# Attention by values and its output transposes as 64x64 products in four places of the array

## The chip, the cores and the metric

The kernel runs on one core of one Trainium2 chip. The metric is the device time of one execution in microseconds. TensorE (PE in the profile) multiplies; VectorE (DVE), ScalarE (ACT) and GpSimd (POOL) work on SBUF and PSUM; SyncE (SP) issues the data transfers.

## What is computed

A delta-rule recurrence over 768 positions for 4 batches of 8 heads of dimension 48, and behind it a causal softmax attention with four experts (head dimension 64), whose outputs are mixed by a top-2 gate:

```python
for t in range(S):                       # first stage, k_n is k over its norm
    y[:, :, t] = einsum('bhd,bhde->bhe', q[:, :, t], state)
    v_old = einsum('bhde,bhd->bhe', state, k_n[:, :, t])
    state += beta[t] * outer(k_n[:, :, t], v[:, :, t] - v_old)
x = y with the heads side by side        # 4 x 768 x 384
for e in range(4):                       # second stage
    q, k, v = x @ wq[e], x @ wk[e], x @ wv[e]
    a = softmax(causal(q @ k.T / 8))
    out += gate[e] * (a @ v @ wo[e])     # gate: top 2 of x @ w_gate, softmax over the two
```

All inputs, and the products that the change touches, are float32.

## The kernel before

The work is cut into six units `n` (0 to 5) of 256 positions of two batches `b`; `s = n % 3` is the place of the unit in its sequence, so that its queries see the keys of `s + 1` units. The recurrence of a unit goes in four chunks of 64 positions, by products of 64x64 or smaller (steps `gk`, `gq`, `ks`, `uu`, `st`, `yq`, `yu`); these already stand in four places of the array, one for each half of its rows and half of its columns, and `turns` puts them in the order (0,0), (1,1), (0,1), (1,0). The triangular solve of each unit (`pre`, `pa`, `sv`; lines L422 and L420 in the profile) is a chain on DVE and POOL.

The attention of unit `n` follows the unit's recurrence and is interleaved with that of the next unit. For a batch `b`, a pair `y` of experts (`x` = 0, 1 within it) and a block `kp` of 256 keys:

- `sc` puts the transposed scores, keys on partitions, into a pair of PSUM banks, with a mask product where `kp == s`;
- `xp` (ACT, L743) takes the exponent into one of three SBUF tiles `at`;
- `av` multiplies by the values `VS`, 64 columns and a column of ones for the row sums, and adds over `kp` in PSUM: 128 keys by 128 queries a product, 65 moving columns. A block below the diagonal has 8 products, a block on it 6. A float32 product leaves two records in the trace, a load and a matmul each;
- `oa`, when all `kp` are done, copies the 128x260 sums from PSUM to `OS` (ACT for e = 0, 13 times; DVE for e = 1, 11 times), and this frees the pair of banks.

When all of a batch's experts are done, `nm` (three small DVE rows on `rsm`) and `on` (POOL or DVE) normalise and gate, `ft` transposes through the array against the identity, `fh` and `fl` evict in two parts, `fo` multiplies by `wo`, `eo` evicts and `do` stores.

PSUM is four pairs of two banks, `PP[0]` to `PP[3]` (`ps_65` to `ps_68` in the order of instructions). `two(k)` is pair `k`, with the bank as its second index. The order of all steps, and the pair or engine that each uses, is written out by hand in the table `ORDER`; every engine runs its own steps in that order, and waits on semaphores for the others.

Of the kernel before, what the change touches and what calls it, by code (L numbers as in the profile page):

```python
# [12 lines left out]
OP = mybir.AluOpType  # L13
# [10 lines left out]
SIDES = (slice(0, 64), slice(64, 128))  # L24
# [148 lines left out]
def tile_kernel(ctx, tc, kq, kv, beta, wqk, wvg, wo, consts, out):  # L173
    nc = tc.nc
    V, S, G, T = nc.vector, nc.scalar, nc.gpsimd, nc.tensor
# [5 lines left out]
    def mm(o, a, b, start, stop=True):  # L181
        T.matmul(o, lhsT=a, rhs=b, start=start, stop=stop, skip_group_check=True)  # L182

    def cpy(e, o, x, scale=None):
        if e == 0:
            S.activation(o, x, AF.Copy, **({} if scale is None else {"scale": scale}))  # L186
        elif scale is None:
            V.tensor_copy(o, x)
        else:
            V.tensor_scalar(o, x, scale, None, op0=OP.mult)  # L190
# [6 lines left out]
    def two(k):  # L197
        return PP[int(k)]
# [15 lines left out]
    id64 = cst[:, 0:64]  # L214
# [19 lines left out]
    VS = cp.tile([128, 2, 6, NE, EH + 1], F32, name="vs")  # L234
# [11 lines left out]
    OS = [cp.tile([128, NE, 2, EH + 1], F32, name=f"os{i}") for i in range(2)]  # L246
    ON = cp.tile([128, 2, NE, EH], F32, name="on")
# [415 lines left out]
    FOUR = ((0, 0), (1, 1), (0, 1), (1, 0))  # L663
# [81 lines left out]
    def av(n, b, y, kp, k):  # L745
        s = n % 3
        A = at_of(n, b, y, kp)
        O = two(k)[:, 0, 0:260].rearrange("p (x i d) -> p x i d", x=2, i=2)
        for j in range(2):
            for x in range(2):  # L750
                for i in range(j if kp == s else 0, 2):
                    o = 256 * j + 128 * i - (128 if kp == s and j else 0)
                    mm(O[:, x, i], A[:, x, o:o + 128], VS[:, b, 2 * kp + j, 2 * y + x], kp == j == x == i == 0)

    def oa(n, b, y, e, k):
        cpy(e, OS[b][:, 2 * y:2 * y + 2].rearrange("p x i d -> p (x i d)"), two(k)[:, 0, 0:260])

    def nm(n, b):
        rs = rsm[:, b]
# [8 lines left out]
    def ft(n, b, k):  # L768
        for i in range(2):
            for x in range(2):  # L770
                for r in range(2):
                    w = 128 * i + 64 * x
                    mm(two(k)[:, r, w:w + 64], ON[SIDES[r], i, 2 * x:2 * x + 2].rearrange("p e d -> p (e d)"), id64[SIDES[r]], True)

    fv = lambda k: two(k)[:, :, 0:256].rearrange("p r (q t) -> p q r t", q=4)
    ov = lambda x: x.rearrange("p i x (r t) -> p (i x) r t", r=2)
# [103 lines left out]
```

## Time and profile before

| | |
|---|---|
| median of 3 runs | 488.77 us (484.72 to 489.02) |
| the profiled execution's own time | 488.29 us |
| its span, first to last instruction | 486.4 us |
| mean granted TensorE clock | 0.959 |
| PE busy | 433.9 us, 89% |
| weight loads (PEld) busy | 396.1 us, 81% |
| DVE busy | 313.6 us, 64% |
| ACT, POOL busy | 182.3 us and 170.8 us |
| the chain that ended last | PE 71%, DVE 15%, DMA 4%, ACT 4% |

Busy time on PE is the union of matmuls from start to modelled end, so that short products that overlap count once, and the last one's latency counts in full. A row of the kind "x44, 5.13" in the timeline is 44 such records that follow each other. "Idle before" with "issue" as its releaser is a stop for which the trace shows no semaphore.

### The profile page before, as it was taken

To read this page: it belongs to the slowest core of one execution; us is meant where nothing else is said; L and a number is where in the kernel's file an instruction comes from. 1 tells how busy PE (TensorE), PEld (TensorE's weight loads), DVE (VectorE), ACT (ScalarE), POOL (GpSimd) and SP (SyncE) were. 2 spreads that over 40 slices of the span, in tenths; PEclk is the share of its full clock that TensorE was granted. 3 is DMA by queue.
4 is the path that set the end of the run, shared out by engine and by line. 5 is a ranking of instruction groups with operands and counts; after the bars stand their busy time and mean duration, and the time that the engine had idled before them with its cause. 6 is when DMAs were issued, how large, how long until landed. Compare 5 with 4: busy or idle time off the path is not lost.

```text
span 486.4 us, 21099 instructions
## 1 busy us (share of the span) xinstructions
PE 433.9 (89%) x9543; PEld 396.1 (81%) x9543; DVE 313.6 (64%) x655; ACT 182.3 (37%) x349; POOL 170.8 (35%) x314
## 2 busy tenths in 40 slices
PE   5529888878999889998999999999999989999995
PEld 4529777867888769897888989999887879999994
DVE  3996769766679894776667485775677764642011
ACT  2516233532325542364352354173531122323331
POOL 1505744544474462404146342744601000011000
PEclk9999999868999996998699999999999989999999
DMA  8920343211303151120035120011403000000001
GB/s 187 236 71 13 91 119 102 49 36 47 105 11 107 34 167 52 52 67 1 3 100 150 35 53 1 1 36 37 144 16 110 19 3 18 2 34 15 20 1 66
DMA packets 15435, 29.33 MB, mean 60 GB/s; under 512 B 2801, under 2 KB 8945, under 8 KB 15345
## 3 DMA queue, kind: packets, MB, share of 16 engines
q1 hardware_dynamic: 15088, 27.59, 20.7%
q8 instruction: 75, 1.23, 1.1%
q10 hardware_dynamic: 256, 0.39, 0.3%
q14 instruction: 16, 0.12, 0.1%
HBM read 20.89 MB, written 4.72 MB: 53 GB/s over the span
## 4 chain that ended last, share of the span: by engine, by line
PE 71%; DVE 15%; DMA 4%; ACT 4%; issue 3%; SPq 1%; POOL 1%; DVEq 0%; ACTq 0%; POOLq 0%
PE ps L182 71%; DMA at<-in_wvg_dram 2%; ACT tt L186 1%; DVE bl L420 1%; DVE mx L684 1%; DVE tp L422 1%; DMA kq<-in_kq_dram 1%; DMA kv<-in_kv_dram 1%; DVE tn L452 1%; DVE ql L619 1%; SPq L596 1%; DMA xh<-xh 1%; DVE tt L190 1%; DVE xb L538 1%; DVE xh L590 1%
## 5 line engine op out<-in xcount | busy, mean ns | idle before, releaser
L182 PE MATMUL ps<-vs,at 128*128 128x65 f32 x672 | 80.1, 276 | 0.1
L182 PEld LDWEIGHTS ps<-vs,at 128*128 128x128 f32 x672 | 77.3, 192 | 1.8 <-ACT at L743 0.4
L422 POOL TENSOR_TENSOR tp<-bl 128x238 f32<-128x238 f32 (+13 forms) x90 | 44.0, 489 | 89.3 <-DVE bl L420 80.6
L743 ACT ACTIVATE at<-ps 128x768 f32<-128x768 f32 (+1 forms) x48 | 43.8, 919 | 50.0 <-PE ps L182 49.8
L684 DVE TENSOR_REDUCE mx<-ps 128x2 f32<-128x1024 f32 (+3 forms) x48 | 44.8, 952 | 13.9 <-PE ps L182 13.6
L420 POOL TENSOR_TENSOR bl<-bl,tp 128x238 f32<-128x238 f32 (+13 forms) x90 | 47.1, 523 | 7.1
L182 PE MATMUL ps<-kq 48*64 48x64 f32 x1536 | 38.2, 243 | 12.0 <-DVE tt L348 4.8
L182 PE MATMUL ps<-xh,wqkh 128*128 128x256 f32 x288 | 45.5, 294 | 2.9 <-DMA xh<-xh 1.8
L182 PEld LDWEIGHTS ps<-kq 48*64 48x64 f32 x1536 | 32.4, 154 | 16.0 <-issue 6.6
L182 PEld LDWEIGHTS ps<-xh,wqkh 128*128 128x128 f32 x288 | 38.6, 194 | 4.9 <-issue 2.0
L186 ACT ACTIVATE tt<-ps 32x256 f32<-32x256 f32 (+2 forms) x87 | 33.4, 384 | 17.1 <-PE ps L182 10.7
L182 PE MATMUL ps<-qh,kh 64*128 64x256 f32 x192 | 35.1, 357 | 1.1 <-DVE sb L562 1.1
L182 PE MATMUL ps<-kh,qh 64*128 64x512 f32 (+3 forms) x128 | 26.8, 439 | 3.5 <-DVE kl L619 2.1
L182 PE MATMUL ps<-ql,kh 64*128 64x256 f32 x192 | 28.2, 285 | 0.0
L182 PEld LDWEIGHTS <-ide 64*128 64x128 bf16 (+1 forms) x479 | 23.3, 103 | 5.9 <-issue 1.2
L182 PE MATMUL ps<-qh,kl 64*128 64x256 f32 x192 | 28.0, 283 | 0.0
L182 PE MATMUL ps<-mr,sel 64*128 64x256 bf16 x192 | 27.3, 276 | 0.0
L182 PE MATMUL ps<-wvgh,xh 128*128 128x260 f32 x144 | 25.4, 303 | 1.4 <-DVE pm L356 1.4
L182 PE MATMUL ps<-mask,ide 64*128 64x128 bf16 (+1 forms) x384 | 26.4, 217 | 0.0
L765 POOL TENSOR_TENSOR on<-os,rsm 128x512 f32<-128x512 f32 x9 | 9.4, 1048 | 46.1 <-DVE rsm L762 46.1
L182 PE MATMUL ps<-xh,wqkl 128*128 128x256 f32 x144 | 25.4, 286 | 0.0
L182 PEld LDWEIGHTS ps<-wvgh,xh 128*128 128x128 f32 x144 | 21.2, 204 | 2.0 <-DVE pm L356 1.6
(197 smaller groups left out, 915.9 us busy)
## 6 DMA issues: line engine op xcount, KB each, us to landing
kv<-in_kv_dram SPq DMA_DIRECT2D x24, 384.0 KB, 3.7
kq<-in_kq_dram SPq DMA_DIRECT2D x40, 192.0 KB, 3.6
out_dram<-ot SPq DMA_DIRECT2D x12, 384.0 KB, 2.9
xh<-xh SPq DMA_DIRECT2D x72, 32.0 KB, 2.5
kq<-in_kq_dram SPq DMA_DIRECT2D x12, 96.0 KB, 3.9
at<-in_wqk_dram SPq DMA_DIRECT2D x3, 256.0 KB, 3.8
kq<-in_kq_dram ACTq DMA_DIRECT2D x4, 96.0 KB, 4.0
at<-in_wvg_dram SPq DMA_DIRECT2D x1, 256.0 KB, 7.6
```

The costliest lines, as they stand in the source:

```text
L182: T.matmul(o, lhsT=a, rhs=b, start=start, stop=stop, skip_group_check=True)
L186: S.activation(o, x, AF.Copy, **({} if scale is None else {"scale": scale}))
L190: V.tensor_scalar(o, x, scale, None, op0=OP.mult)
L420: e.tensor_tensor(X[:, a:b, i + 1:], X[:, a:b, i + 1:], tv, op=OP.subtract)
L422: e.tensor_tensor(tv, R[:, :, i + 1:].to_broadcast([128, w, m]), X[:, a:b, i:i + 1].to_broadcast([128, w, m]), op=OP.mult)
L452: V.transpose(TN[n % 2].rearrange("p t l -> p l t"), BB[n % 2])
L538: V.tensor_tensor(XB.rearrange("p (a b) d -> p a (b d)", a=2), kv_of(n, c)[:, 1].rearrange("p (a b) d -> p a (b d)", a=2), ax(k), op=OP.su ...
L590: V.tensor_tensor(x, y, yv(n, c, k, 0)[0], op=OP.subtract)
L596: nc.sync.dma_start(x[r + HD:r + 64, :, i].bitcast(F32), x[r + 16 * i:r + 16 * i + 16, :, 3].bitcast(F32))
L684: V.tensor_reduce(d, two(k)[:, :, a:a + 128 * (k1 - k0)], axis=AX.X, op=OP.max)
L743: S.activation(at_of(n, b, y, kp)[:, :, 0:w], two(k)[:, :, 0:w], AF.Exp, scale=0.125)
L765: (V, G)[e - 1].tensor_tensor(ON, OS[b][:, :, :, 0:EH].rearrange("p e i d -> p i e d"), rsm[:, b, :, :, None].to_broadcast([128, 2, NE, EH ...
```

## The change

`av` cuts each 128x128 product into four of 64x64: key half `r` (rows of the array) by query half `c` (its columns). The two key halves go to the two banks of the pair, so both banks now hold a partial sum. On a diagonal block the products whose key half lies above the query half are left out, except in units 0 and 3, where one of each pair is still needed to write the region. The products of the four places take turns, in the same order of places as `turns` has. `oa` copies bank 0 as before, on the engine that it had, and then adds bank 1 on DVE. `ft` takes a 64x64 piece at a time where it took 64x128. `ORDER` is as it was.

```diff
     def av(n, b, y, kp, k):
         s = n % 3
         A = at_of(n, b, y, kp)
-        O = two(k)[:, 0, 0:260].rearrange("p (x i d) -> p x i d", x=2, i=2)
-        for j in range(2):
-            for x in range(2):
-                for i in range(j if kp == s else 0, 2):
-                    o = 256 * j + 128 * i - (128 if kp == s and j else 0)
-                    mm(O[:, x, i], A[:, x, o:o + 128], VS[:, b, 2 * kp + j, 2 * y + x], kp == j == x == i == 0)
+        O = two(k)[:, :, 0:260].rearrange("p r (x i d) -> p r x i d", x=2, i=2)
+        todo = {}
+        for x in range(2):
+            for j in range(2):
+                for i in range(2):
+                    for r in range(2):
+                        for c in range(2):
+                            if kp == s and 2 * j + r > 2 * i + c and (s or j):
+                                continue
+                            todo.setdefault((r, c), []).append((x, j, i))
+        seen = set() if kp == 0 else {(r, c) for r in range(2) for c in range(2)}
+        while any(todo.values()):
+            for r, c in ((0, 0), (1, 1), (0, 1), (1, 0)):
+                if not todo[r, c]:
+                    continue
+                x, j, i = todo[r, c].pop(0)
+                o = 256 * j + 128 * i + 64 * c - (128 if kp == s and j else 0)
+                mm(O[SIDES[c], r, x, i], A[SIDES[r], x, o:o + 64], VS[SIDES[r], b, 2 * kp + j, 2 * y + x], (r, c) not in seen)
+                seen.add((r, c))
 
     def oa(n, b, y, e, k):
-        cpy(e, OS[b][:, 2 * y:2 * y + 2].rearrange("p x i d -> p (x i d)"), two(k)[:, 0, 0:260])
+        o = OS[b][:, 2 * y:2 * y + 2].rearrange("p x i d -> p (x i d)")
+        cpy(e, o, two(k)[:, 0, 0:260])
+        V.tensor_tensor(o, o, two(k)[:, 1, 0:260], op=OP.add)
...
     def ft(n, b, k):
         for i in range(2):
             for x in range(2):
-                for r in range(2):
+                for r, c in FOUR:
                     w = 128 * i + 64 * x
-                    mm(two(k)[:, r, w:w + 64], ON[SIDES[r], i, 2 * x:2 * x + 2].rearrange("p e d -> p (e d)"), id64[SIDES[r]], True)
+                    mm(two(k)[SIDES[c], r, w:w + 64], ON[SIDES[r], i, 2 * x + c], id64[SIDES[r]], True)
```

On PE, in the second expert pair of batch 0 and the first of batch 1 of the last unit, `av` of three key blocks stands in a row (here a product counts once, not twice as in the trace; `at_112` to `at_114` are the three exponent tiles, `ps_66` and `ps_67` two pairs of banks):

```order
 L182 MATMUL ps_68<-mr_86,sel 128x256
-L182 MATMUL ps_66<-vs,at_113 128x65 x8
-L182 MATMUL ps_66<-vs,at_114 128x65 x6
-L182 MATMUL ps_67<-vs,at_112 128x65 x8
+L182 MATMUL ps_66<-vs,at_113 64x65 x32
+L182 MATMUL ps_66<-vs,at_114 64x65 x20
+L182 MATMUL ps_67<-vs,at_112 64x65 x32
 L182 MATMUL ps_65<-qh_100,kh 128x256 x2
```

22 products become 84 in the same place between the same neighbours; nothing is moved.

On DVE, at the end of the program, the last two `oa` of batch 1 (`os_119`) and what waits behind them; L771 is the new addition:

```order
 L188 COPY os_119<-ps_67 128x260
+L771 TENSOR_TENSOR os_119<-os_119,ps_67 128x260
 L188 COPY ot<-ps_67 128x768
 L188 COPY os_119<-ps_68 128x260
-L760 TENSOR_SCALAR rsm<-os_119 128x8
-L761 RECIPROCAL rsm<-rsm 128x8
-L762 TENSOR_TENSOR rsm<-gt_127,rsm 128x8
-L765 TENSOR_TENSOR on<-os_119,rsm 128x512
+L771 TENSOR_TENSOR os_119<-os_119,ps_68 128x260
+L775 TENSOR_SCALAR rsm<-os_119 128x8
+L776 RECIPROCAL rsm<-rsm 128x8
+L777 TENSOR_TENSOR rsm<-gt_127,rsm 128x8
```

The additions stand directly behind the copies, ahead of the small rows of `nm` (L775 to L777, before L760 to L762).

On DVE, in the middle of the program, the row of unit 0 where one of the two evictions was ACT's (`os_118` from `ps_65`), between the copy and the solver's rows:

```order
 L188 COPY os_118<-ps_67 128x260
+L771 TENSOR_TENSOR os_118<-os_118,ps_67 128x260
+L771 TENSOR_TENSOR os_118<-os_118,ps_65 128x260
 L422 TENSOR_TENSOR tp<-bl_94 128x238
 L420 TENSOR_TENSOR bl_94<-bl_94,tp 128x17x14
```

DVE had no row for the eviction from `ps_65`; it now has one, which waits for the copy by ACT, with the solver's rows (L422, L420) queued behind it.

## The prediction

> **What bounds the kernel now.** I read the page first: which engine is busy, and what the chain that ended last is made of.
>
> ```profile
> PE 433.9 (89%) x9543; PEld 396.1 (81%) x9543; DVE 313.6 (64%) x655; ACT 182.3 (37%) x349; POOL 170.8 (35%) x314
> q8 instruction: 75, 1.23, 1.1%
> PE 71%; DVE 15%; DMA 4%; ACT 4%; issue 3%; SPq 1%; POOL 1%; DVEq 0%; ACTq 0%; POOLq 0%
> L182 PE MATMUL ps<-vs,at 128*128 128x65 f32 x672 | 80.1, 276 | 0.1
> ```
>
> The products by values are PE's costliest group, 80.1 us. An average over 486 us says little about what they are worth, so I then asked for the busy time by stretches, of all engines, and of these products alone:
>
> ```profile
> 0.00:240.00 240.00, 199.78 (x5026) 179.66 (x5030) 176.28 (x360) 96.73 (x206) 106.48 (x197) 0.93 0.30 79
> 240.00:300.00 60.00, 58.24 (x1302) 54.16 (x1294) 39.50 (x91) 24.94 (x44) 26.23 (x51) 1.00 0.25 69
> 300.00:400.00 100.00, 94.96 (x2314) 86.36 (x2313) 69.87 (x146) 35.06 (x66) 31.52 (x48) 0.98 0.16 45
> 400.00:480.00 80.00, 78.70 (x913) 74.05 (x910) 27.38 (x59) 24.80 (x34) 6.55 (x18) 1.00 0.06 19
> ...
> 0.00:240.00 240.00, 22.95 (x324) 0.93 0.30 79
> 240.00:300.00 60.00, 18.82 (x160) 1.00 0.25 69
> 300.00:400.00 100.00, 11.44 (x92) 0.98 0.16 45
> 400.00:480.00 80.00, 33.97 (x288) 1.00 0.06 19
> ...
> 399.95 76.08 PE ps L182 x880
> 476.06 0.44 DVE os L188
> ```
>
> Columns are length, then busy time and count of PE, PEld, DVE, ACT, POOL, then clock and transfers. The last two rows are from the chain in order of time. From 400 us on PE is the bound without a break: 76 us of the chain are PE alone, and DVE has 27 us to do in 80. Here a microsecond saved on PE is one saved at the end. Before 240 us PE is busy 200 of 240 and DVE 176: recurrence and solver wait for each other, and PE is not what ends last for long. (Of the 324 there, 192 are set-up products that also read `vs`; 132 are ours.)
>
> **What a product costs, before and after.** From the timeline:
>
> ```profile
> 264.01 5.12 PE L182 MATMUL ps<-vs,at 128*128 128x65 f32 x44
> ...
> 253.60 0.66 PE L182 MATMUL ps<-pm,ub 64*48 64x64 f32 x32
> 254.09 0.54 PE L182 MATMUL ps<-ub,kv 64*48 64x48 f32 x32
> ```
>
> The 44 records take (5.12 - 0.28)/43 = 113 ns each, with the last one's 0.28 us (the group's mean) taken off. The 32 records of `yu` stand in the four places already, with 64 columns; from their start to the next step's is 0.49 us, 15.3 ns a record, 61 ns a round of four. A record of before becomes one round: a block below the diagonal has 16 records and gets 16 rounds, a block on it 12 and 12 (some rounds of three). So 672 x (113 - 61) = 35 us of PE time go. The price of the 65th column and of rounds of three is not in the trace; between 58 and 66 ns a round it moves the sum by 3 us.
>
> The Trainium skill, page "TensorE: Matmul & The Clock Gate", section "Wait — 56ns, not 53.3ns?", states a rule against this: start-to-start of matmuls never drops below about 25 ns. By it the 2528 new records would take 63 us for 76 and the change would save 13 us of PE, not 35. The trace's 15.3 ns disagrees, and I go by the trace.
>
> `ft` has 8 products, in two halves of the rows:
>
> ```profile
> 250.51 1.08 PE L182 MATMUL ps<-cst,on 64*128 64x64 f32 x16
> L538 DVE TENSOR_TENSOR xb<-kv,ps 128x384 f32<-128x384 f32 x22 | 12.0, 546 | 3.9 <-PE ps L182 3.1 <-ACT pm L355 0.4 <-DMA kv<-in_kv_dram 0.3
> L188 DVE COPY os<-ps 128x260 f32<-128x260 f32 x11 | 4.7, 424 | 16.9 <-PE ps L182 16.7
> L186 ACT ACTIVATE os<-ps 128x260 f32<-128x260 f32 x13 | 5.0, 387 | 30.6 <-PE ps L182 29.1 <-POOL tp L422 1.5
> ```
>
> (1.08 - 0.28)/15 = 53 ns a record now, 2 x 15.3 = 31 ns then: 16 x 0.022 = 0.36 us off each of 12 steps, of which four lie between 400 and 480 us. The added DVE row reads PSUM and SBUF. It lies between the copy of its own size, 0.39 to 0.42 us, and the subtraction on 384 columns, 0.55; I take 0.42, and 24 of them are 10 us of DVE. From 400 us on DVE is idle two thirds of the time and hides all but the last one, which stands on the chain at 476.06 and adds 0.45 us; the last `ft` gives 0.36 back. Before 240 us eight of them (units 0 and half of 1, 3.4 us) stand in DVE's queue ahead of the solver, and those behind an ACT copy also wait for it there.
>
> **What the added records cost elsewhere.** The queue named "instruction" moved 1.23 MB in 75 packets, 16.4 KB each; the page counts 2 x 9543 = 19086 records on PE, so a packet is about 256 PE instructions. One piece of the timeline shows what that means:
>
> ```profile
> 255.52 0.64 PE L182 MATMUL ps<-kq 48*64 48x64 f32 x29 [0.41 <-issue]
> 255.98 0.20 PE L182 MATMUL ps<-sb,kq 48*64 48x48 f32 x1
> 255.98 0.23 PE L182 MATMUL ps<-kq 48*64 48x64 f32 x3
> 256.03 0.64 PE L182 MATMUL ps<-sb,kq 48*64 48x48 f32 x31
> 256.60 0.61 PE L182 MATMUL ps<-woh,oh 128*128 128x384 f32 x2
> 257.05 0.51 PE L182 MATMUL ps<-wol,oh 128*128 128x384 f32 x2
> 257.40 0.51 PE L182 MATMUL ps<-woh,ol 128*128 128x384 f32 x2
> 257.84 0.66 PE L182 MATMUL ps<-kq,sb 48*48 48x64 f32 x32
> 258.43 0.34 PE L182 MATMUL ps<-ide 128*128 128x192 bf16 x2
> 258.70 0.56 PE L182 MATMUL ps<-xb,tt 64*64 64x48 f32 x24
> 259.52 0.33 PE L182 MATMUL ps<-xb,tt 64*64 64x48 f32 x8 [0.26 <-issue]
> ```
>
> PE stops twice in the middle of a step, for no semaphore. Between the stops lie 29 + 1 + 3 + 31 + 2 + 2 + 2 + 32 + 2 + 24 = 128 matmuls, with their loads 256 instructions, and 4.00 us. I read this as: **a block of 128 matmuls cannot be fetched in less than about 4.0 us**, and four-place records use one up in 128 x 15.3 ns = 1.96 us. The change adds 1856 + 192 = 2048 matmuls, 16 blocks to 75, all of them dense. By stretch, with the records of our products going from 160 to 608, 92 to 344 and 288 to 1088, and those of `ft` (32, 64 and 64) doubled:
>
> - 240 to 300: 1302 + 448 + 32 = 1782 matmuls, 13.9 blocks, 56 us at least. PE alone would need 60 - 8.3 - 0.7 = 51. Fetching is the new bound, and as dense steps stand in clusters, worse than the mean: I take 58, so -2 (bounds -9 and +4).
> - 300 to 400: 2314 + 252 + 64 = 2630, 20.5 blocks, 82 us of 100. PE saves 4.8 + 1.4, part of it in waits for DVE: -2 (bounds -6 and +2).
> - 400 to 480: 913 + 800 + 64 = 1777, 13.9 blocks, 56 us; PE needs 80 - 15.0 - 1.4 = 63.6. The mean fits, the clusters do not: the last unit's four sets of 84 products are 168 matmuls, 1.3 blocks, done in 2.6 us. Where a whole block falls within one, up to 2 us are lost; I take 1.25 each, 5 in all (bounds 0 and 8). So -16.4 + 5 = -11.4.
> - before 240: 132 x 52 = 6.9 us of PE time, against 3.4 us of DVE rows in front of the solver and dense steps that already meet the fetching limit: 0 (bounds -5 and +4).
>
> **The clock.** Windows of 3.4 us around the places where the granted clock (third column from the right) falls to half:
>
> ```profile
> 88.41:91.83 3.42, 1.64 (x70) 1.00 0.38 90
> 91.83:95.24 3.41, 3.28 (x15) 0.50 0.17 52
> 115.72:119.14 3.42, 2.09 (x129) 1.00 0.05 10
> 224.95:228.36 3.41, 1.89 (x17) 1.00 0.00 0
> 228.36:238.60 10.24, 10.13 (x156) 0.50 0.01 2
> ```
>
> After a window with PE busy 1.64 or 1.89 us of 3.4 the clock is halved for 3.4 or 10.2 us; after 2.09 of 3.4 it is not. Stops of up to 2 us in every 4 bring windows near that edge. A halved stretch of 10.2 us full of PE work loses up to 5.1 us. I count one more of them than before: +5.
>
> **Sum**: -11.4 - 2 - 2 + 0 + 0.1 (the end) + 5 = -10.3 us against the profiled execution's 488.29, which is 0.5 us under the median of the three runs: **478 us**.
>
> **Rivals.**
>
> 1. *Fetching stays hidden*, because PE's queue runs far enough ahead in the slow score products between the clusters. For it: from 400 to 480 us 913 matmuls take 80 us, 88 ns each, so that the steps between the clusters use up few instructions and leave time to fetch. Against it: a cluster of 1.3 blocks is longer than what can have been fetched ahead, if the two stops above are a guide. Then the stretches give -16.4, -5 and -2, with no 5 for stops and none for the clock: 465.
> 2. *The clock eats the gain*: the stops put two more stretches at half clock than forecast, both full of PE work: 478 + 9 = 487, no change. For it: the edge lies between 1.89 and 2.09 us busy, and a stop of 1.5 to 2 us in each 4 comes to just that. Against it: the two stops above, 0.41 and 0.26 us, fell into a stretch with the clock at 1.00 throughout. The Trainium skill's page "TensorE: Matmul & The Clock Gate", section "HAM oscillation — how this bites in real kernels", asks for an idle gap above some 3.4 us; by it no stop of 2 us would cost clock and this rival would not exist. The row 88.41 disagrees: 1.64 us busy of 3.42 leaves no gap above 1.8, and the clock fell.
> 3. *Slower, by the fetching limit*: if a block takes longer when the recurrence's transfers share the same engines (transfer share 0.25 in 240 to 300). At T us a block, 240 to 400 needs 34.4 T against 160 before, and decides against the change from T = 4.65 there, sooner with clusters. At 5.0 it is 12 us longer; the end of the program gains 4 (its 13.9 blocks take 70, clusters take the rest to 76), one halved stretch costs 5: 488 - 4 + 12 + 5 = 501. Against it: both stops above are 4.00 us apart although two kinds of transfers were under way.
> 4. *The places do not run side by side here*, because the accumulation or the two banks serialise them. At twice the round, 122 ns, PE gains nothing, and part of the DVE rows before 240 us stays: 490. Against it: `yu` accumulates on sums of `yq` too, at 61 ns. By the skill's floor of 25 ns, quoted above, the round would be 100 ns and the time some 483, between this rival and the forecast.
>
> **Chances**: the forecast (470 to 484) 0.47, rival 1 0.20, rival 2 0.19, rival 3 0.07, rival 4 0.07. About 1%, 4.9 us, is what a measurement can tell from no change. Faster by more takes the first two but a tail: 0.65; within 1% rival 2, most of rival 4 and that tail: 0.26; slower 0.09. The range leaves out rival 3, the rest of rival 4 and the lower half of rival 1: 465 to 490.
>
> **What would show it.** The products by values as 2528 records of 64x65, some 15 ns apart within a step; 91 packets in the instruction queue; stops put down to "issue", 4.0 us and 128 matmuls apart, inside them between 240 and 300 us and after 440; L771 24 times at some 0.42 us; PE still the chain from 390 us on. Wrong it would be if these stops are missing (then 465), if records in a step stand 25 ns or more apart, or if the clock is at half for 20 us more than before.

## The result, and the profile after

The changed kernel takes 470.32 us in the median of its runs (464.38 to 470.76), the kernel before, beside it on the same chip, 487.78 us (484.72 to 489.02): ratio 0.962, 95% interval 0.953 to 0.971, 17.5 us less. A second measurement gave 467.59 beside 484.94, ratio 0.959 (0.951 to 0.967). The forecast was 478, range 465 to 490. Here and below a median is that of all runs, and a ratio with its interval comes from those runs alone that the chip's slower state did not touch, so where the two disagree the ratio decides.

The page of the profiled execution (470.76 us, span 469.0), its engines, the queue that brings instructions, the chain, and the two groups that the change made or added:

```profile
PE 401.6 (86%) x11591; PEld 361.6 (77%) x11591; DVE 319.3 (68%) x679; ACT 181.9 (39%) x349; POOL 171.6 (37%) x314
q8 instruction: 91, 1.49, 1.3%
PE 66%; DVE 15%; issue 6%; ACT 5%; DMA 4%; POOL 2%; SPq 2%; DVEq 0%; ACTq 0%; POOLq 0%
L182 PE MATMUL ps<-vs,at 64*64 64x65 f32 x2528 | 46.2, 220 | 5.0 <-issue 4.9
...
L771 DVE TENSOR_TENSOR os<-os,ps 128x260 f32<-128x260 f32 x24 | 10.1, 423 | 14.5 <-ACT os L186 14.0
```

PE has 32 us less to do (433.9 before), of which 17.4 arrive at the end of the span. The products by values fell from 80.1 to 46.2 us busy, but now PE stands idle ahead of them for 4.9 us with "issue" as the releaser, where all its idle time was 0.1, and "issue" has grown from 3% to 6% of the chain.

To see where the time came from, fixed points in the work are better than fixed times. I take three starts among the 48 exponents (L743 on ACT), which stand in the same order in every kernel: the 11th, the 27th and the last. Each kernel has three rows: the group with its first and last start, then the 11th and the 27th from the timeline. Before, then after:

```profile
L743 ACT ACTIVATE at<-ps x48: 807/918/1033, 120.9 to 470.7; 128x768 f32<-128x768 f32 x24, 128x1024 f32<-128x1024 f32 x24
216.85 0.81 ACT L743 ACTIVATE at<-ps 128x768 f32<-128x768 f32 x1 [0.31 <-PE ps L182]
329.27 0.81 ACT L743 ACTIVATE at<-ps 128x768 f32<-128x768 f32 x1 [0.73 <-PE ps L182]
```

```profile
L743 ACT ACTIVATE at<-ps x48: 805/918/1032, 121.9 to 453.0; 128x768 f32<-128x768 f32 x24, 128x1024 f32<-128x1024 f32 x24
215.68 0.81 ACT L743 ACTIVATE at<-ps 128x768 f32<-128x768 f32 x1 [0.31 <-PE ps L182]
324.44 0.81 ACT L743 ACTIVATE at<-ps 128x768 f32<-128x768 f32 x1 [0.74 <-PE ps L182]
```

The **first part**, up to the 11th exponent, went from 216.8 to 215.7; the **middle**, from there to the 27th, from 112.4 to 108.8; the **last part**, to the last exponent, from 141.4 to 128.6; what follows, from 15.7 to 16.0. So 12.8 of the 17.4 us come from the last part, and the middle, which has many products by values too, gave 3.7.

What stands in the middle, from PE's timeline (all rows with a stop put down to "issue" between 240 and 287 us, with two rows ahead of the longest):

```profile
240.29 0.51 PE L182 MATMUL ps<-cst,on 64*64 64x64 f32 x18 [0.66 <-issue]
251.76 0.40 PE L182 MATMUL ps<-kq 48*64 48x64 f32 x12 [1.00 <-issue]
...
258.96 0.66 PE L182 MATMUL ps<-kq 48*64 48x64 f32 x32
259.52 2.37 PE L182 MATMUL ps<-vs,at 64*64 64x65 f32 x145
265.17 0.63 PE L182 MATMUL ps<-vs,at 64*64 64x65 f32 x21 [3.28 <-issue]
...
277.81 0.59 PE L182 MATMUL ps<-pm,ub 64*48 64x64 f32 x26 [0.90 <-issue]
281.82 0.39 PE L182 MATMUL ps<-qh,kl 64*128 64x256 f32 x2 [0.18 <-issue]
285.83 1.38 PE L182 MATMUL ps<-vs,at 64*64 64x65 f32 x79 [1.14 <-issue]
```

These stops add up to 7.2 us. They wait for no semaphore that the trace shows, and they come in the middle of a step: 277.81, 281.82 and 285.83 lie 4.01 us apart. The rate between them is the forecast one: 145 records in 2.37 us, less the last one's 0.22, are 15 ns each.

### The profile page after: what moved, and what is told of

The parts are those of the page before. It is cut to its first block, busy times and chain, and to the rows that moved or that the text cites. A ratio compares the mean times of both kernels' runs of the same rounds, so it can differ in the third digit from the quotient of the medians.

```text
span 469.0 us, 25214 instructions
## 1 busy us (share of the span) xinstructions
PE 401.6 (86%) x11591; PEld 361.6 (77%) x11591; DVE 319.3 (68%) x679; ACT 181.9 (39%) x349; POOL 171.6 (37%) x314
## 4 chain that ended last, share of the span: by engine, by line
PE 66%; DVE 15%; issue 6%; ACT 5%; DMA 4%; POOL 2%; SPq 2%; DVEq 0%; ACTq 0%; POOLq 0%
PE ps L182 66%; DMA at<-in_wvg_dram 2%; ACT tt L186 1%; DVE mx L684 1%; DVE ql L619 1%; DVE tn L452 1%; SPq L596 1%; DMA vs<-in_consts_dram 1%; DVE tt L190 1%; DMA xh<-xh 1%; DVE xb L538 1%; DVE os L771 1%; DMA kq<-in_kq_dram 1%; ACT qh L186 1%; DVE bl L420 1%
## 5 line engine op out<-in xcount | busy, mean ns | idle before, releaser
L422 POOL TENSOR_TENSOR tp<-bl 128x238 f32<-128x238 f32 (+13 forms) x90 | 44.1, 490 | 85.8 <-DVE bl L420 65.5
L743 ACT ACTIVATE at<-ps 128x768 f32<-128x768 f32 (+1 forms) x48 | 43.9, 919 | 44.9 <-PE ps L182 44.7
L182 PE MATMUL ps<-vs,at 64*64 64x65 f32 x2528 | 46.2, 220 | 5.0 <-issue 4.9
L420 POOL TENSOR_TENSOR bl<-bl,tp 128x238 f32<-128x238 f32 (+13 forms) x90 | 47.4, 527 | 7.1
L182 PEld LDWEIGHTS ps<-vs,at 64*64 64x64 f32 x2528 | 42.2, 135 | 8.0 <-issue 6.5
L182 PE MATMUL ps<-kh,qh 64*128 64x512 f32 (+3 forms) x128 | 25.6, 423 | 3.7 <-DVE kl L619 2.1
L182 PEld LDWEIGHTS ps<-qh,kh 64*128 64x128 f32 x192 | 20.1, 205 | 4.3 <-DVE os L771 2.8
```

The source lines that it names most:

```text
L420: e.tensor_tensor(X[:, a:b, i + 1:], X[:, a:b, i + 1:], tv, op=OP.subtract)
L422: e.tensor_tensor(tv, R[:, :, i + 1:].to_broadcast([128, w, m]), X[:, a:b, i:i + 1].to_broadcast([128, w, m]), op=OP.mult)
L743: S.activation(at_of(n, b, y, kp)[:, :, 0:w], two(k)[:, :, 0:w], AF.Exp, scale=0.125)
```

## Experiments

The words "first, middle and last part" are those of the section above, and the numbers behind them come from the same three starts in each kernel's trace.

**The products by values alone, and the transposes alone.** `e1_av_only` keeps the old `ft`, `e2_ft_only` the old `av` and `oa`:

```diff
 e1_av_only, against the changed kernel
-                for r, c in FOUR:
+                for r in range(2):
-                    mm(two(k)[SIDES[c], r, w:w + 64], ON[SIDES[r], i, 2 * x + c], id64[SIDES[r]], True)
+                    mm(two(k)[:, r, w:w + 64], ON[SIDES[r], i, 2 * x:2 * x + 2].rearrange("p e d -> p (e d)"), id64[SIDES[r]], True)
 e2_ft_only, against the kernel before: the same lines the other way round
```

> The changed products by values and their addition, with the output transposes as they were before. All theories: nearly the whole gain stays, since the transposes are worth at most 12 x 0.36 = 4 us. Theory 1 (35 us of PE time saved, part of it given back to stops for instructions and to the additions): 472 us. If the transposes carried more than their PE time (by freeing a pair of banks sooner): above 476.

> Only the output transposes change, the products by values are as before. Theory 1: -1 to -3 us, 485 to 487, hardly to be told from no change. The stops for instructions grow by little, 192 matmuls more are 1.5 blocks.

Measured: 469.55 us, ratio 0.968 (0.949 to 0.987), and 485.60, ratio 1.004 (0.997 to 1.010). The effect is that of `av` and `oa`; the transposes carry nothing that these times can tell from nothing.

**Column halves alone.** `e3_cols` splits each product by its query columns only: all 128 keys, 64 columns, two places, one bank. There is no addition, and `ft` is the old one.

```diff
-                    mm(O[:, x, i], A[:, x, o:o + 128], VS[:, b, 2 * kp + j, 2 * y + x], kp == j == x == i == 0)
+                    for c in range(2):
+                        mm(O[SIDES[c], x, i], A[:, x, o + 64 * c:o + 64 * c + 64], VS[:, b, 2 * kp + j, 2 * y + x], kp == j == x == i == 0)
```

> The products by values are split by the halves of the array's columns alone (128 keys by 64 queries, two places), so there is one bank and no addition on DVE, and 1344 records in place of 672, not 2528; transposes as before. Theory 1: the price of a record is its weight load, 64 columns for 128, so two places give the same PE time as four: 57 to 61 ns a pair of records. With half the new instructions and no addition the stops between 240 and 300 us shrink to about half and the time falls to about 463 us, 7 below the changed kernel. Rival 2 (four places are needed for the speed, two give half of it): 57 ns a record, no PE time saved, 486 us. Rival 3 (the clock sets what is left): within 3 us of the changed kernel, 467 to 473.

Measured: 451.54 us, ratio 0.931 (0.913 to 0.948), beyond what any theory had. I ran it again beside the changed kernel on one chip (`e11_cols_again` and `e12_after_again`, the same two kernels):

> The products by values split by column halves only (two places, one bank, no addition, old transposes), once more, beside the changed kernel on the same chip. If the first measurement of it holds: 451 us, between 446 and 458, ratio to before 0.92 to 0.95, and 4% under the changed kernel. If it was a lucky session: 460 or more.

> The changed kernel itself, in the same session: 470 us, between 465 and 474, ratio 0.95 to 0.97.

Measured: 455.85 us, ratio 0.941 (0.936 to 0.947), and 467.59 for the changed kernel. So half of the split, with 672 new records for the products where all of it has 1856, is better than all of it: by 12 us in the medians, by 9 in the ratios, whose intervals do not overlap (the changed kernel's is 0.951 to 0.967). I had expected 4% between them; it is 2 to 2.5%. The rows of the products and of the instruction queue in the first trace, and the exponents in the first and in the second:

```profile
L182 PE MATMUL ps<-vs,at 128*64 128x65 f32 x1344 | 46.5, 227 | 0.0
...
q8 instruction: 80, 1.31, 1.2%
...
L743 ACT ACTIVATE at<-ps x48: 807/916/1032, 125.6 to 443.2; 128x768 f32<-128x768 f32 x24, 128x1024 f32<-128x1024 f32 x24
219.68 0.81 ACT L743 ACTIVATE at<-ps 128x768 f32<-128x768 f32 x1 [0.30 <-PE ps L182]
315.74 0.81 ACT L743 ACTIVATE at<-ps 128x768 f32<-128x768 f32 x1 [0.74 <-PE ps L182]
```

```profile
L743 ACT ACTIVATE at<-ps x48: 809/918/1031, 120.8 to 435.7; 128x768 f32<-128x768 f32 x24, 128x1024 f32<-128x1024 f32 x24
211.19 0.81 ACT L743 ACTIVATE at<-ps 128x768 f32<-128x768 f32 x1 [0.30 <-PE ps L182]
308.16 0.81 ACT L743 ACTIVATE at<-ps 128x768 f32<-128x768 f32 x1 [0.74 <-PE ps L182]
```

Two places with one bank bring PE's busy time for these products to the same 46 us as four places with two. "Issue" no longer ends a wait of these matmuls, and 80 packets of instructions are moved instead of 91. Middle and last part take 96.1 and 127.5 us, and in the repeat 97.0 and 127.5, against 108.8 and 128.6 of the changed kernel (105.4 and 128.6 in its repeat). So the last part is worth the same to about a microsecond in both, and the middle is 8 to 13 us shorter with columns alone. The first part differs by 8 us between two executions of the very same kernel; no difference of a few us there can be read from one profile.

The granted clock is part of these differences. Here is the middle of the changed kernel, of `e4_no_add`, of the column split and of `e9_cols_max` (the second and fourth are described below); the third number from the right is the clock:

```profile
215.68:324.44 108.76, 98.36 (x2856) 88.81 (x2858) 76.40 (x184) 48.69 (x93) 50.69 (x94) 0.94 0.16 45
209.85:315.68 105.83, 95.73 (x2856) 86.33 (x2858) 76.17 (x176) 48.80 (x94) 50.59 (x94) 0.97 0.16 45
219.68:315.74 96.06, 93.29 (x2384) 84.56 (x2386) 74.76 (x177) 48.73 (x93) 50.60 (x94) 1.00 0.18 50
215.63:316.85 101.22, 97.73 (x2384) 88.52 (x2386) 77.13 (x184) 48.80 (x93) 50.31 (x94) 0.95 0.16 47
```

Length times clock is an estimate of what a stretch would take at full clock, if PE is its bound wherever the clock is low. It gives 102 and 103 us for the two kernels in four places, and 96 and 96 for the two in two places. So about 6 us of the middle belong to the split itself, about what its stops there add up to, and the rest to the clock. The two first parts, 219.7 us at 0.93 and 211.2 at 0.95, come out as 204 and 201, so more than half of their difference is the clock too.

**Row halves alone.** `e10_rows` splits by keys only: 64 keys, 128 columns, two banks and the addition.

```diff
-                    mm(O[:, x, i], A[:, x, o:o + 128], VS[:, b, 2 * kp + j, 2 * y + x], kp == j == x == i == 0)
+                    for r in range(2):
+                        mm(O[:, r, x, i], A[SIDES[r], x, o:o + 128], VS[SIDES[r], b, 2 * kp + j, 2 * y + x], kp == j == x == i == 0)
...
         cpy(e, o, two(k)[:, 0, 0:260])
+        V.tensor_tensor(o, o, two(k)[:, 1, 0:260], op=OP.add)
```

> The products by values split by row halves alone (64 keys by 128 queries, two places, two banks, with the addition on DVE; transposes as before). Theory 1: the weight load of 128 columns still sets the pace, 107 to 113 ns in each of two places, 53 to 57 ns a record as the transposes have it before, so twice the records take the same PE time; with 24 additions and 672 more matmuls the kernel is slower than before by 2 to 10 us, 490 to 498. Rival 2 (any split into two places doubles the rate): 465 to 475.

Measured: 486.75 us, ratio 1.001 (0.993 to 1.008): no change, where I had expected a loss.

```profile
L182 PE MATMUL ps<-vs,at 64*128 64x65 f32 x1344 | 80.1, 273 | 0.1
L182 PEld LDWEIGHTS ps<-vs,at 64*128 64x128 f32 x1344 | 77.2, 188 | 2.1 <-issue 0.8
```

Twice as many records, and the busy time is 80.1 us as before, 60 ns a record for 119, so that the two row halves give nothing. Of the two cuts only the one by columns, which leaves 64 weight columns to load instead of 128, shortens PE's work: its weight loads are busy for 42.7 us, those of the row halves for 77.2. That the loads set the pace is the likely reason, and no run tries it by itself.

**Without the additions.** `e4_no_add` is the changed kernel without L771; what half of the keys contribute to the output is left out.

```diff
         cpy(e, o, two(k)[:, 0, 0:260])
-        V.tensor_tensor(o, o, two(k)[:, 1, 0:260], op=OP.add)
```

> The changed kernel without the addition of the second bank on DVE, so the sums leave out half of the keys. Theory 1 says the additions cost some 5 to 10 us by holding pairs of banks and by standing in DVE's queue ahead of other rows, and the stops for instructions stay: 461 to 465, with stops between 240 and 300 us of 6 us or more in sum. Rival 2 (the additions lie beside other work but for the last): 469 to 470.

Measured: 462.00 us, ratio 0.957 (0.945 to 0.969), within the first theory's 461 to 465: some 6 to 8 us under the changed kernel by the medians, but by the ratios (0.962 and 0.959 there) only 1 to 2. The counterpart, `e9_cols_max`, gives the column split a row of the same form and operands, one that leaves the sums as they are:

```diff
         cpy(e, o, two(k)[:, 0, 0:260])
+        V.tensor_tensor(o, o, two(k)[:, 0, 0:260], op=OP.max)
```

> The column split, and behind each eviction copy a DVE row of the same form and operands as the addition of the changed kernel, but taking the larger of the copied sums and the same bank, which leaves them as they are. 24 rows of about 0.42 us. Theory: the additions cost by lying on DVE ahead of the solver's rows and by holding the bank, whatever TensorE's records look like: 7 to 9 us over the column split, 458 to 461. Rival: they cost only together with the stops of the four-place records, which leave no slack: 0 to 3 us over it, 451 to 454.

Measured: 461.77 us, ratio 0.944 (0.934 to 0.954). That is 5.9 us over the column split by the medians, between what the two theories had, but 1 us by the ratios (0.944 and 0.941), with intervals that overlap. The exponents without the additions, in the four places:

```profile
L743 ACT ACTIVATE at<-ps x48: 805/915/1032, 120.2 to 445.1; 128x768 f32<-128x768 f32 x24, 128x1024 f32<-128x1024 f32 x24
209.85 0.81 ACT L743 ACTIVATE at<-ps 128x768 f32<-128x768 f32 x1 [0.30 <-PE ps L182]
315.68 0.81 ACT L743 ACTIVATE at<-ps 128x768 f32<-128x768 f32 x1 [0.74 <-PE ps L182]
```

Middle and last part take 105.8 and 129.4 us, no less than with the additions (105.4 to 108.8 and 128.6): behind the 11th exponent the additions cost nothing that can be seen in the four places. What they cost would then lie in the first part, 209.9 here and 215.7 and 219.7 with them; but that part also came out as 219.7 and 211.2 in two profiles of the column split, which has no addition.

The clock settles most of this. For each kernel, the mean of span times granted clock over the runs that its ratios use and whose clock is on record (the same estimate as above, over the whole span):

| kernel | runs | span x clock, us |
|---|---|---|
| before | 19 | 469 |
| row halves | 6 | 470 |
| column halves | 8 | 438 |
| column halves with the row of `e9_cols_max` | 2 | 442 |
| four places without additions (`e4_no_add`) | 3 | 444 |
| four places (the changed kernel) | 7 | 445 |

The times of the 19 runs of before lie between 478 and 486 us with clocks of 0.965 to 0.986, and the products between 467 and 472, so this takes out part of what scatters. By it the additions cost 1 us in the four places, and in the column split 4, from two runs; and the row halves, which have the 24 additions too, are no slower than before. The 6 to 8 us between the medians are for the most part clock; whether the additions have a part in the lower clock is not shown. What the additions do hold up can be seen in the changed kernel's trace:

```profile
208.88 0.39 PE L182 MATMUL ps<-qh,kh 64*128 64x256 f32 x2 [1.72 <-DVE os L771]
316.67 0.38 PE L182 MATMUL ps<-qh,kh 64*128 64x256 f32 x2 [0.53 <-DVE os L771]
321.82 0.67 PE L182 MATMUL ps<-kq,sb 48*48 48x64 f32 x32 [0.86 <-DVE os L771]
```

These are 3.1 us of PE's waits, the longest of them in the first part; in the last part none reaches 0.2 us.

**How fast instructions come.** `e5_probe` is the kernel before with three dense runs at its end, which feed nothing: 512 float32 and 1024 bf16 products in the four places, then 512 products of 128x64 in two places. (The bf16 loop, left out below, is the first one with `idb` and twice the turns.) In this trace a bf16 product too leaves a load and a matmul.

```diff
+        for i in range(32):
+            for _ in range(4):
+                for r, c in FOUR:
+                    mm(two(k)[SIDES[c], r, 0:64], id64[SIDES[r]], id64[SIDES[r]], True)
...
+        for i in range(32):
+            for _ in range(4):
+                for c in range(2):
+                    mm(two(k)[SIDES[c], 0, 128:192], AT[0][:, 0, 64 * c:64 * c + 64], id64, True)
```

> The kernel before with three dense runs of products behind the last store, whose results nobody reads: 512 float32 products 64x64 in four places (1024 matmul records), 1024 bfloat16 products 64x64 in four places (1024 records), 256 float32 products of 128 rows by 64 columns in two places (512 records). If PE's instructions come in blocks of 256 with about 4.0 us a block at the least, the first run takes 8 x 4.0 = 32 us with a stop every 128 matmuls, and the second takes the same 32 us although its records are a quarter as long or less; the third, 512 records, 4 blocks, 16 us or its PE time of 512 x 29 = 15 us. If there is no such limit, the first takes 1024 x 15.3 = 15.7 us and has no stops, the second at most 10 us.

Measured, from PE's timeline (start, duration, records, stop ahead):

```profile
479.85 3.72 PE L182 MATMUL ps<-cst 64*64 64x64 f32 x239
485.65 2.09 PE L182 MATMUL ps<-cst 64*64 64x64 f32 x128 [2.07 <-issue]
489.67 2.09 PE L182 MATMUL ps<-cst 64*64 64x64 f32 x128 [1.93 <-issue]
493.41 2.09 PE L182 MATMUL ps<-cst 64*64 64x64 f32 x128 [1.65 <-issue]
...
516.43 1.93 PE L182 MATMUL ps<-ide 64*64 64x64 bf16 x128 [2.11 <-issue]
520.45 1.92 PE L182 MATMUL ps<-ide 64*64 64x64 bf16 x128 [2.09 <-issue]
524.20 1.92 PE L182 MATMUL ps<-ide 64*64 64x64 bf16 x128 [1.82 <-issue]
...
539.27 16.92 PE L182 MATMUL ps<-cst,at 128*64 128x64 f32 x512
```

PE works off 128 records in 2 us, and then stops until 3.74 to 4.02 us have gone by, whatever the type. This is the rate in the long run: the first 239 records, behind slower products, ran through in 3.72 us without a stop, so about a block must have stood ready by then. The third run needs 33 ns a record, 4.2 us for 128, and has no stop at all. That is why the column split has few stops in the products by values: in the middle part of five profiles with column halves all stops put down to "issue" add up to 0 to 1.4 us, in that of five profiles with four places to 6.8 to 8.0. A record of before becomes two of 33 ns, 66 ns, hardly more than a round of four in 61, but with half as many instructions.

**The same kernel with its block boundaries moved.** `e6_phase` puts 64 small products, 128 PE instructions, at the start of the changed kernel, far from the path.

```diff
+    def pad():
+        for _ in range(64):
+            mm(two(3)[:, 1, 320:336], ide[:, 0:128], ide[:, 0:16], True)
```

> The changed kernel with 64 short bfloat16 products (64 matmuls and 64 loads, half a block of instructions) ahead of the work, while PE waits for the first inputs. If the stops belong to the boundaries of blocks of 256 instructions, each moves by half a block: the stop of 3.28 us inside the products by values at 265 us and the others fall into other steps, 128 instructions (64 matmuls) earlier in the program; the time may move by 3 us to either side. If the stops belong to the steps in which they stand (a late input, a bank), they stay where they are and the time stays within 1 us, 470.

Measured: 473.50 us, ratio 0.977 (0.967 to 0.988), 3 us over the changed kernel by the medians. Its stops between 259 and 288 us:

```profile
262.52 2.76 PE L182 MATMUL ps<-vs,at 64*64 64x65 f32 x85 [2.40 <-issue]
273.14 1.15 PE L182 MATMUL ps<-vs,at 64*64 64x65 f32 x57 [0.33 <-issue]
276.87 0.56 PE L182 MATMUL ps<-ub,kv 64*48 64x48 f32 x28 [1.56 <-issue]
284.62 0.57 PE L182 MATMUL ps<-vs,at 64*64 64x65 f32 x20 [1.29 <-issue]
```

In the cluster with the longest stop, 85 records now stand behind it where 21 did, 64 more, as many as were put ahead. The stops keep to a count of instructions and not to a step.

**Better versions.** `e7_cols_ft` is the column split with the new `ft`; `e8_cols_ft_fill` has, besides, 20 and 12 filling products for 8 and 8 in the last two waits of `ORDER`:

```diff
-nm.5.1 on.5.1.1 fill.8:1 ft.5.1:1
-fh.5.1.0:1 fl.5.1:1 fill.8:0 fo.5.1.0:0
+nm.5.1 on.5.1.1 fill.20:1 ft.5.1:1
+fh.5.1.0:1 fl.5.1:1 fill.12:0 fo.5.1.0:0
```

> The split by column halves alone for the products by values, with no addition, and the output transposes in four places as in the changed kernel. Theory 1: about 1 to 2 us under the split by columns with the old transposes, 461 us; a gain under 1 us would say that the transposes lie beside other work.

> The column split with the new transposes, and longer filling products in the two waits at the end of the program (20 for 8 and 12 for 8), so that the window ahead of the last projection stays busy and the granted clock does not fall there. Theory: the halved clock at the end costs 1 to 2 us where it falls, so 1 to 2 us under the column split with the new transposes (455.3 in its own session, 451 to 456). Rival: the filling delays the products behind it by as much: no change.

Measured: 455.30 us, ratio 0.940 (0.931 to 0.949), and 454.62, ratio 0.937 (0.930 to 0.945). Neither can be told from the column split's 455.85 (0.941). By span times clock the new transposes are worth 1 to 3 us in each of three pairs (437 for 438 here), as far as such an estimate goes. The column split beats both kernels, by 29 us the one before.

## Why the prediction was right, and where its sum was not

**What a product costs: right.** The rate of 15.3 ns a record was forecast, 15 came. The busy time of these products fell by 33.9 us for 35 forecast, PE's in all by 32.3. The rule quoted there from the Trainium skill, page "TensorE: Matmul & The Clock Gate", section "Wait — 56ns, not 53.3ns?", that starts of matmuls never lie under about 25 ns apart, does not hold in this trace for products that alternate between four places: `x145` in 2.37 us, and 128 in 2.09 in the probe.

**The fetching limit: right in kind.** 91 packets came; the stops lie where a block of 128 matmuls ends, 4.0 us apart in the dense places, and the probe shows the block by itself, at 3.74 to 4.02 us. What the prediction left out of its sum, and named only under rival 1, is the reserve: behind slower work a cluster longer than a block runs through without a stop, as the probe's first 239 records do, and 168 at 274.06 us of the changed kernel, in 2.75 us.

**Where the stops fall: the term that was mis-sized.** For the last stretch I took four losses of 1.25 us, 5 in all. The last part shows these, and one of 0.29 us at 339:

```profile
330.96 0.69 PE L182 MATMUL ps<-kq,sb 48*48 48x64 f32 x28 [1.95 <-issue]
...
442.35 0.86 PE L182 MATMUL ps<-vs,at 64*64 64x65 f32 x43 [0.28 <-issue]
449.58 1.05 PE L182 MATMUL ps<-vs,at 64*64 64x65 f32 x57 [0.23 <-issue]
```

From 400 us on 0.5 us were lost, not 5: there rival 1 was right, and the slow score products between the clusters are the likely reason. With the boundaries 64 products further on, `e6_phase` has a last part of 134.6 us, 6 more: its stops there add up to 6.2 us for 2.8, and its clock is 0.97 for 0.99. So the small loss is in part a matter of where the boundaries happen to fall. The last part gained 12.8 us, about what the forecast had for it (11.4 from 400 us on, and up to 1.4 of the 2 for 300 to 400 us). That the sums agree owes something to luck: PE was busy 15.7 us less in that part (136.4 to 120.7) where the sum took 16.4 and more, and it lost 2.8 to stops where the sum took 5 and more.

Rival 1 was priced too high at 465. It takes 5 and 2 us from the two stretches between 240 and 400 us, for which the prediction itself names 9 and 6.2 us of PE time saved; with these it would have been 457. The column split, which has next to no stops in these products, came to 452 to 456.

**The middle: right in kind.** For 240 to 300 us I took 2 us of gain for 9 of PE time saved, and the middle, which is longer, gave 3.7, in the repeat 7.1. The column split, with the same busy time for these products and next to no such stops, gives 15 to 16. At full clock, by the estimate above, it is 5 for the one (107 to 102) and 10 to 11 for the other. One block there took 5.4 us instead of 4.0. Stretches of both kinds:

```profile
259.80:265.20 5.40, 2.12 (x145) 1.98 (x136) 1.96 (x5) 0.00 (x0) 3.89 (x10) 1.00 0.51 161
281.80:285.80 4.00, 2.88 (x128) 2.65 (x128) 3.90 (x6) 2.08 (x3) 2.56 (x3) 1.00 0.25 57
```

The transfer share (last column but one) was 0.51 in the long one and 0.25 in the other. Rival 3 supposed that transfers lengthen a block, but one such pair does not show it, and other blocks speak against it: in the kernel before, 59.80 to 63.80 and 63.80 to 67.80 us are blocks of 4.00 us with shares of 0.41 and 0.40, and the same block in the repeat took 4.5 us with 0.28. The cause of the long block stays open.

**Before 240 us: open.** I had 0, of PE time against additions. The first part came out at -1.2 and, in the repeat, +2.9, within what one and the same kernel varies there. (Of the additions seven, not eight, start before 240 us.)

**The clock: right in sign.** Two windows in which the granted clock fell, each followed by its halved stretch:

```profile
263.07:266.49 3.42, 1.32 (x84) 1.32 (x87) 0.49 (x2) 0.11 (x1) 1.18 (x3) 1.00 0.04 9
266.49:273.32 6.83, 6.83 (x108) 6.22 (x100) 4.52 (x13) 3.41 (x7) 1.29 (x2) 0.50 0.24 60
...
457.70:461.12 3.42, 1.73 (x42) 1.36 (x42) 1.71 (x6) 0.60 (x1) 0.00 (x0) 0.99 0.17 61
461.12:464.54 3.42, 3.42 (x12) 3.40 (x11) 0.48 (x1) 0.00 (x0) 0.00 (x0) 0.51 0.00 0
```

The first holds the end of the stop of 3.28 us; the stretch behind it is full of PE work and costs up to 3.4 us. The mean clock went from 0.959 to 0.948 in the two profiles: 2 x 0.041 x 486 = 40 us at half clock before, 2 x 0.052 x 469 = 49 after, 9 more, worth up to 4.5 us for the 5 forecast. Over the runs of the table above, span less span times clock is 12 us before and 20 after, so the clock took 8 us back, more than forecast. That the stops cause it was not tried. Rival 2 asked for two more such stretches than that and did not come. The rule of the Trainium skill quoted with it, from the same page, section "HAM oscillation — how this bites in real kernels", wants an idle gap above some 3.4 us; in the second window, row 457.70, the longest stop of PE is 1.68 us, so the trace speaks against it once more.

**What the prediction did not see.** It weighed the change as one thing. The gain belongs to the cut by columns, and the cut by rows takes part of it back: 1184 records more, which bring the stops, and a bank more, which brings the additions. By the medians, from the kernel before at about 486 us: column halves 452 to 456, four places without additions 462, with them 468 to 470. By span times clock, where the clock's share is out of it: 31 us less for the column halves, 6 to 7 more for the row halves on top without additions, 1 more for the additions. The forecast gain was 10 us and the measured one 17.5: the stretches gave 24 us at full clock where the sum took 15, and the clock took 8 back where it took 5.

## What to carry to other kernels

Ask which cut of a product shortens PE's work, and make that one alone: here halving the weight columns brought it all, and halving the rows brought instructions, a second bank and an addition. Count PE instructions per microsecond where dense steps follow each other for several blocks: there 128 records took 3.7 to 4.0 us here, so records closer than some 30 ns gain nothing; a single cluster behind slower work ran through. Where single executions scatter, compare between fixed points of the work, and multiply each length by its granted clock before a difference of a few microseconds is put down to an edit.

## What had not been expected of the hardware

In a run of dense products a block of 256 PE instructions took 3.74 to 4.02 us from stop to stop, the same for float32 and bf16; about a block stood ready behind slower work (239 records in 3.72 us). The probe's two-place products (128 rows, 64 columns, float32) start 33 ns apart, so that two places carry nearly as much as four: 66 ns against 61 for the work of one 128x128 record. Two row halves of 64x128 took as long as one product of 128x128 (80.1 us busy both). And a window of 3.42 us with PE busy for 1.73 us, half of it, was followed by a halved clock (row 457.70).
